# Seven token tiles instead of eight in the first phase of an attention and two-layer kernel, with fewer buffers

## The chip, the cores and the metric

The kernel runs on one core of one Trainium2 chip. The metric is the device time of one execution in microseconds (us), the median of three runs; a profiled execution of its own gives the trace.

## What is computed

The reference in short (float32 in and out; D = 64, 8 heads, 4 batches of 768 positions, so 3072 tokens of 512 values):

```python
for c in range(S // 32):                       # chunks of 32 positions
    k_full = concat(mem_k, k[32c - 16 : 32c + 40])   # 8 memory tokens, 16 left, 8 right
    v_full = concat(mem_v, v[32c - 16 : 32c + 40])
    a = softmax(q_c @ k_full.T / sqrt(64))
    out[32c : 32c + 32] = a @ v_full
x = out as (3072, 512)
h = x @ w_in                                   # 512 -> 2048
g = max(h, 0) + log1p(exp(-abs(h)))            # softplus
x1 = g @ w_out                                 # 2048 -> 512
y = ((x1 @ w_a) * (x1 @ w_b)) @ w_out2         # 512 -> 1536 -> 512
```

## The kernel before, in words

Every matrix product of the two layers is made of three: each operand is split into a high half (rounded to the type that TensorE takes at its full rate) and the low half that is left, and high*high, high*low and low*high are added up.

**Phase 1** makes x1 in token tiles of 384 (`TT`), eight of them. A tile has 16 steps f, one for each 128 columns of w_in. `emit_h` (L563) makes h of the step in 12 matmuls of 384 columns into one of two PSUM banks `ph`. `emit_soft` makes softplus of it: Abs, Exp and Ln on ACT (L570 to L572) in a tile `e`, the sum with max(h, 0) on DVE (L574) into `g`, a ring of two; then `split` writes the high half gh on ACT (L551) and the low half gl on POOL (L554; in the first and the last tile on DVE), each in a ring of three. Two steps later (`LAG`) `emit_x1` (L587) multiplies gh and gl with w_out in 12 matmuls, which add into four accumulator banks `px`. So PE's order is h(f), x1(f-2), h(f+1), x1(f-1), and the last two steps of a tile are multiplied when the next tile's h(0) and h(1) have been made. After the last x1 of a tile the four accumulators are copied to SBUF (L595, tiles `xo`, of which two come from the ring `g`) and stored (L596); the next tile's first product into a bank has to wait for that bank's copy.

**Attention** is done in units of 128 tokens that are woven into phase 1. A unit's steps are: turn (transposes of k and q on DVE, L411 to L414, with copies on ACT), scores (32 small matmuls, L430), soft (eight DVE instructions L379 with eight exps on ACT, L383), norm (DVE L387, L388, then POOL L390), flip and flip2 (five DVE transposes each, L448), values (32 small matmuls, L477) and place (its halves to the x tile, ACT L484 and DVE L485). Each step is put at a slot, a half of a step f, so that a tile has 32: `PLACED` gives the slots at which the three units of a tile have their values, and the other steps are counted from there. The loads of k and q (`HALVES`) are counted from the turns.

**Order.** PE, DVE and SP run in the order in which the program is written out (`order`, `att_at`). ACT and POOL run in the written order in the first and the last tile, and in between in an order that a scheduler chooses. In phase 1 weights of phase 2 are prepared too (`Early`, `Conversion`): `PRE` says how many of such jobs a tile takes.

**Phase 2** works on three pairs of 512 tokens twice, 12 steps each, with seven products of sums (L772, six matmuls of 512 columns each), whose results DVE combines in temporaries q, r and d21 (L824 to L864) in `pair_step`, and the second product as jobs (L795). The first products of phase 2 stand between the last two x1 of phase 1: pX, pY, x1(14), pW, x1(15), pV. pV goes into the bank of the first accumulator. The sums of tokens that the products read (`operand`, `split_hi`, `split_lo`, L652, L656) are in tiles that take over memory of phase 1.

## Time and profile before

| | |
|---|---|
| median of 3 runs | 1172.94 us (1171.99 to 1175.8) |
| the profiled execution's own time | 1173.41 us |
| its span | 1171.6 us |
| PE busy | 1161.1 us, 99% of the span, 7462 instructions |
| DVE busy | 724.2 us, 62% |
| ACT busy | 530.7 us, 45% |
| POOL busy | 263.6 us, 23% |
| chain that ended last | PE 94%, DMA 2%, DVE 1% |

The page gives the busy time of each engine, and the chain of waits says which engine each moment of the span waited for. A matmul is shown with the time until its result is in PSUM, which is longer than the time until the next one may start: the distance of matmuls that follow each other is read from a run of them in the chain. Between two tiles or at the start of a stage the timeline says which instruction ended what wait.

### The profile page before, as it was taken

What the parts mean: (1) busy time and instruction counts of PE and PEld (TensorE: products, weight loads), DVE (VectorE), ACT (ScalarE), POOL (GpSimd) and SP (SyncE); (2) the same over time, 40 slices, a digit from 0 to 9 for tenths busy, and PEclk for the clock granted to TensorE, in tenths of its full rate; (3) what the DMA queues carried; (4) which work ended last, traced back from release to release, by engine and by line L of the source; (5) the groups of instructions that cost most, each with busy time, mean ns of one, the idle gap of its engine ahead of it and who ended that gap; (6) DMA issues with size and microseconds to landing.
All of it is one profiled execution on the core that took longest, in us unless ns stands there. A gap on an engine that the chain in (4) does not pass through costs nothing.

```text
span 1171.6 us, 20283 instructions
## 1 busy us (share of the span) xinstructions
PE 1161.1 (99%) x7462; PEld 1049.1 (90%) x7462; DVE 724.2 (62%) x1603; ACT 530.7 (45%) x1293; POOL 263.6 (23%) x239
## 2 busy tenths in 40 slices
PE   9899999999999999999999999999999999999998
PEld 7799999999999999999999888888888888888887
DVE  6888655565555655455377567867456657455555
ACT  6899666656666566666565332222211113111110
POOL 2000223233232222322324665710002001000000
PEclk9999999999999999999999999999999999999999
DMA  9955353533534335332474758464854443864301
GB/s 228 301 189 103 90 135 76 132 80 98 132 79 125 81 104 136 75 101 68 140 261 161 274 216 287 171 224 150 339 203 144 152 145 106 305 226 153 135 1 72
DMA packets 193714, 181.47 MB, mean 155 GB/s; under 512 B 123168, under 2 KB 151760, under 8 KB 193616
## 3 DMA queue, kind: packets, MB, share of 16 engines
q1 hardware_dynamic: 193232, 180.13, 49.4%
q8 instruction: 59, 0.97, 0.3%
q14 instruction: 39, 0.32, 0.1%
q0 software_dynamic: 384, 0.05, 0.0%
...
## 4 chain that ended last, share of the span: by engine, by line
PE 94%; DMA 2%; DVE 1%; SPq 1%; ACT 0%; issue 0%; POOL 0%; DVEq 0%; POOLq 0%
PE px L587 22%; PE ph L563 22%; PE py L795 17%; PE pX L772 8%; PE pV L772 8%; PE pW L772 8%; PE pY L772 4%; PE pxa L477 2%; PE sc L430 1%; DMA raw<-in_moe_w_in_dram 1%; DMA vv<-in_v_dram 1%; DMA kp<-in_k_dram 1%; SPq L330 1%; DVE af L448 0%; PE pa L466 0%
## 5 line engine op out<-in xcount | busy, mean ns | idle before, releaser
L563 PE MATMUL ph<-x,w 128*128 128x384 f32 x1536 | 289.4, 336 | 0.1
L587 PE MATMUL px<-gh,w 128*128 128x384 f32 x1024 | 281.5, 335 | 1.4 <-DVE qn L295 1.4
L563 PEld LDWEIGHTS ph<-x,w 128*128 128x128 f32 x1536 | 267.2, 188 | 2.1 <-ACT x L369 0.2
L795 PE MATMUL py<-w2o,c 128*128 128x512 f32 (+1 forms) x870 | 218.0, 388 | 0.0
L795 PEld LDWEIGHTS py<-w2o,c 128*128 128x128 f32 x870 | 162.7, 188 | 33.5
L587 PEld LDWEIGHTS px<-gh,w 128*128 128x128 f32 x1024 | 186.7, 188 | 2.8 <-DVE qn L295 1.8
L574 DVE SCALAR_TENSOR_TENSOR g<-ph,e 128x384 f32<-128x384 f32 x128 | 71.0, 555 | 189.0 <-ACT e L572 184.9
L587 PE MATMUL px<-gl,w 128*128 128x384 f32 x512 | 171.1, 334 | 0.0
L854 ACT CAST c<-r 128x512 fp32r<-128x512 f32 x36 | 22.4, 622 | 308.2 <-DVE r L852 287.2
L554 POOL TENSOR_TENSOR gl<-g,gh 128x384 fp32r<-128x384 f32 x96 | 97.3, 1014 | 222.8 <-ACT gh L551 206.7
L551 ACT CAST gh<-g 128x384 fp32r<-128x384 f32 x128 | 65.6, 513 | 88.4 <-DVE g L574 87.2
L804 DVE TENSOR_TENSOR y<-py,y 128x512 f32<-128x512 f32 (+1 forms) x121 | 82.9, 685 | 36.2 <-PE py L795 36.0
L570 ACT ACTIVATE e<-ph 128x384 f32<-128x384 f32 x128 | 62.3, 486 | 88.4 <-PE ph L563 75.7
L587 PEld LDWEIGHTS px<-gl,w 128*128 128x128 f32 x512 | 96.1, 188 | 0.1
L448 DVE STREAM_TRANSPOSE af<-sm 32x256 f32<-32x256 f32 x180 | 78.2, 434 | 3.6 <-POOL sm L390 1.1
L572 ACT ACTIVATE e<-e 128x384 f32<-128x384 f32 x128 | 67.3, 526 | 3.9
L571 ACT ACTIVATE e<-e 128x384 f32<-128x384 f32 x128 | 67.3, 526 | 3.6
L851 DVE TENSOR_TENSOR d<-pW,q 128x512 f32<-128x512 f32 x36 | 24.9, 691 | 69.1 <-PE pW L772 69.1
L383 ACT ACTIVATE sm<-sm,st 128x96 f32<-128x96 f32 x168 | 60.5, 363 | 5.8 <-DVE st L379 5.8
L772 PE MATMUL pX<-x,u 128*128 128x512 f32 x216 | 54.8, 389 | 0.0
L772 PE MATMUL pW<-xs,u 128*128 128x512 f32 x216 | 54.8, 389 | 0.0
L772 PE MATMUL pY<-xs,u 128*128 128x512 f32 x216 | 54.8, 389 | 0.0
...
## 6 DMA issues: line engine op xcount, KB each, us to landing
...
```

Of the source, the lines that this page charges most:

```text
L448: nc.vector.transpose(out=af[32 * kb:32 * kb + 32, x], in_=self.sm[32 * x:32 * x + 32, :, 32 * kb:32 * kb + 32])
L551: anchor[0] = nc.scalar.copy(hi, val)
L554: engine.tensor_tensor(lo, val, hi.bitcast(F32), ALU.subtract)
L563: nc.tensor.matmul(ph, lhsT=w[:, a, kt * P:(kt + 1) * P], rhs=x[:, c, kt, :], start=n == 0, stop=n == 3 * KT - 1)
L570: nc.scalar.activation(e, ph, AF.Abs)
L571: nc.scalar.activation(e, e, AF.Exp, scale=-1.0)
L572: nc.scalar.activation(e, e, AF.Ln, bias=1.0)
L574: nc.vector.scalar_tensor_tensor(g, ph, 0.0, e, ALU.max, ALU.add)
L587: nc.tensor.matmul(acc[t][i][:, :TT], lhsT=a, rhs=c, start=f == 0 and m == 0, stop=f == NF1 - 1 and m == 2)
L772: nc.tensor.matmul(bank[:, :T2], lhsT=u[:, j, a, kt * P:kt * P + P], rhs=x[kt][:, c], start=first_ and m == 0, stop=m == 3 * KH - 1, skip_ ...
L795: nc.tensor.matmul(b, lhsT=c[:, x, r], rhs=w[:, y, cols], start=n == 0, stop=n == 3 * GROUP - 1)
L804: tt(y, b, y, ALU.add)
```

## The change

The last 1536 tokens of phase 1 are cut into three tiles of 512 instead of four of 384, so that there are seven tiles. The units get a list of 18 slots with even distances, 9 in the narrow tiles and 8 in the wide ones, and where the distance is under 9 the flips come one slot earlier. Softplus is finished in place in `e`, a ring of two, and `g` is gone; gh and gl are rings of two, and both halves of a step are now made behind x1(f-2), the last reader of the buffers that they take. Of the accumulators' copies two go to the ring `e` and two to a tag that the early jobs use. In phase 2 the sums s1 and 12 share one tile and 22 and s4 another, and the temporaries r and d21 are two halves of a tile `rd` that takes over the memory of the ring gl. `order` splits the sums at other places. The diff, cut to its core:

```diff
 T2 = 512
+WIDTHS = (384, 384, 384, 384, 512, 512, 512)
 
 LAG = 2
-PLACED = (11, 21, 30)
+PLACED = (43, 52, 61, 70, 79, 88, 97, 106, 116, 126, 134, 142, 150, 158, 166, 174, 182, 190)
 TURNED, SCORED = 32, 34
 TURN, SOFT, NORM, FLIP, FLIP2 = -2, 1, 3, 5, 6
-HALVES = ((0, 8, 0.6), (8, 13, 0.9))
+HALVES = ((0, 8, 0.6), (8, 13, 0.8))
 SETS = 1
...
 
-PRE, PRE_BY = 5, 4.2
+PRE, PRE_BY = (0, 5, 5, 6, 7, 7, 0), 4.2
 PRE_STEPS = (0, 3.4, 4.1, 4.3)
...
 
-    masks = [ap.tile([P, KB], F32, name=f"mask{i}") for i in range(4)]
+    masks = [ap.tile([P, KB], F32, name=f"mask{i}") for i in range(3)]
+    masks.append(wp.tile([P, KB], F32, tag="w", name="mask3"))
     ident = wp.tile([P, P], F32, tag="w", name="ident")
...
         if t not in xt:
-            xt[t] = mp.tile([P, 2, KT, TT], F32R, tag="x", name=f"x{t}")
+            xt[t] = mp.tile([P, 2, KT, T2], F32R, tag="x", name=f"x{t}")[:, :, :, :WIDTHS[t]]
         return xt[t]
...
             mask = masks[0 if self.n == 0 else 2 if self.n == NU - 1 else 1]
-            sm = a2.tile([P, H, KB], F32, tag="sm", name=f"sm{u}", bufs=1)
-            st = a2.tile([P, 4, H], F32, tag="st", name=f"st{u}")
+            sm = a2.tile([P, H, KB], F32, tag="kt", name=f"sm{u}", bufs=1)
+            st = a2.tile([P, 4, H], F32, tag="st", name=f"st{u}", bufs=1)
             softmax(self.sc, mask, sm, st)
...
     later = units[UPT:]
-    placed = {u: 2 * NF1 * (u // UPT - 1) + PLACED[u % UPT] for u in range(2 * UPT, len(units))}
+    placed = dict(zip(range(2 * UPT, len(units)), PLACED))
     scored = {u: placed[u - 1] if u > 2 * UPT else SCORED for u in placed}
...
         whens[i] = [(turned[u], "turn"), (at - 0.005, "scores"), (at + SOFT, "soft"), (at + NORM, "norm"),
-                    (max(at + FLIP, to - 7), "flip"), (max(at + FLIP2, to - 5), "flip2"), (to - 0.03, "values"), (to - 0.02, "place")]
+                    (at + FLIP - (to - at < 9), "flip"), (at + FLIP2 - (to - at < 9), "flip2"), (to - 0.03, "values"), (to - 0.02, "place")]
         unit.own_bank = u + 1 < len(units)
...
         if tag not in rings:
-            rings[tag] = mp.tile([P, n, TT], dtype, tag=tag, name=tag, bufs=1)
+            rings[tag] = mp.tile([P, n, T2], dtype, tag=tag, name=tag, bufs=1)
             n_turn[tag] = 0
         n_turn[tag] += 1
         return rings[tag][:, n_turn[tag] % n]
 
-    def split(val, name, engine=nc.gpsimd, between=None):
-        hi, lo = turn_of("gh", 3, F32R), turn_of("gl", 3, F32R)
-        anchor[0] = nc.scalar.copy(hi, val)
-        if between:
-            between()
-        engine.tensor_tensor(lo, val, hi.bitcast(F32), ALU.subtract)
-        return hi, lo
-
     def emit_h(t, f):
         x, w = xt[t], w1[f]
-        ph = ps.tile([P, 512], F32, tag="h", name=f"ph{t}_{f}")[:, :TT]
+        ph = ps.tile([P, 512], F32, tag="h", name=f"ph{t}_{f}")[:, :WIDTHS[t]]
         n = 0
...
     def emit_soft(t, f, ph, engine=nc.gpsimd, one=None, two=None):
-        e = mp.tile([P, TT], F32, tag="e", name=f"e{t}_{f}")
+        c = slice(0, WIDTHS[t])
+        e = turn_of("e", 2, F32)[:, c]
+        hi, lo = turn_of("gh", 2, F32R)[:, c], turn_of("gl", 2, F32R)[:, c]
         nc.scalar.activation(e, ph, AF.Abs)
         nc.scalar.activation(e, e, AF.Exp, scale=-1.0)
         nc.scalar.activation(e, e, AF.Ln, bias=1.0)
-        g = turn_of("g", 2, F32)
-        nc.vector.scalar_tensor_tensor(g, ph, 0.0, e, ALU.max, ALU.add)
+        nc.vector.scalar_tensor_tensor(e, ph, 0.0, e, ALU.max, ALU.add)
         if one:
             one()
-        gt[t, f] = split(g, f"g{t}_{f}", engine, two)
+        gt[t, f] = hi, lo
+
+        def parts():
+            anchor[0] = nc.scalar.copy(hi, e)
+            if two:
+                two()
+            engine.tensor_tensor(lo, e, hi.bitcast(F32), ALU.subtract)
+
+        return parts
 
...
             for m, (a, c) in enumerate(((wh, gh), (wh, gl), (wl, gh))):
-                nc.tensor.matmul(acc[t][i][:, :TT], lhsT=a, rhs=c, start=f == 0 and m == 0,
+                nc.tensor.matmul(acc[t][i][:, :WIDTHS[t]], lhsT=a, rhs=c, start=f == 0 and m == 0,
                                  stop=f == NF1 - 1 and m == 2)
+
+    def emit_x1_out(t, f):
         if f == NF1 - 1:
             for i in range(KT):
+                n = WIDTHS[t]
                 if t == NTILE - 1:
-                    o = wp.tile([P, TT], F32, tag="w", name=f"xo{t}_{i}")
+                    o = wp.tile([P, n], F32, tag="w", name=f"xo{t}_{i}")
+                elif i > 1:
+                    o = mp.tile([P, n], F32, tag="tmp", name=f"xo{t}_{i}", bufs=2)
                 else:
-                    o = turn_of("g", 2, F32) if i > 1 else mp.tile([P, TT], F32, tag="e", name=f"xo{t}_{i}")
-                nc.vector.tensor_copy(o, acc[t][i][:, :TT])
-                nc.sync.dma_start(x1d[:, i, TT * t:TT * t + TT], o)
+                    o = turn_of("e", 2, F32)[:, :n]
+                nc.vector.tensor_copy(o, acc[t][i][:, :n])
+                nc.sync.dma_start(x1d[:, i, C0[t]:C0[t + 1]], o)
             del acc[t]
...
         if n in ("11", "s2", "s3"):
-            return [home(f"x{n}", late["x"], [P, KH, 2, T2], f"x{n}")]
-        if n == "s1":
-            return [home("xs1a", late["x"], [P, 1, 2, T2], "xs1"), home("xa", mp, [P, 3, 2, T2], "x")[:, 0:1]]
-        if n == "12":
-            return [home("xa", mp, [P, 3, 2, T2], "x")[:, 1:3]]
-        if n == "22":
-            return [home("xb", mp, [P, 3, 2, T2], "x")[:, 0:2]]
-        return [parts[p, "xb"][:, 2:3], home("xs4b", mp, [P, 1, 2, T2], "gh")]
-
-    def pieces_of(p, n):
-        k = 0
-        for x in sums[p, n]:
-            yield x, raws[n][:, k:k + x.shape[1]]
-            k += x.shape[1]
-
-    def split_hi(p, n, copy):
-        sums[p, n] = operand(p, n)
-        for x, raw in pieces_of(p, n):
-            copy(x[:, :, 0], raw)
-
-    def split_lo(p, n, engine):
-        for x, raw in pieces_of(p, n):
-            engine.tensor_tensor(x[:, :, 1], raw, x[:, :, 0].bitcast(F32), ALU.subtract)
+            return home(f"x{n}", late["x"], [P, KH, 2, T2], f"x{n}")
+        x = home("xa" if n in ("s1", "12") else "xb", mp, [P, 4, 2, T2], "x")
+        return x[:, 0:2] if n in ("s1", "22") else x[:, 2:4]
+
+    PIECES = {n: 1 for n in PRODUCTS}
+
+    def split_hi(p, n, copy, which=(0, 1)):
+        for i in which:
+            if i < PIECES[n]:
+                x = operand(p, n, i)
+                sums.setdefault((p, n), []).append(x)
+                k = x.shape[1]
+                copy(x[:, :, 0], raws[n][:, i * k:i * k + k])
+
+    def split_lo(p, n, engine, which=(0, 1)):
+        for i in which:
+            if i < PIECES[n]:
+                x = sums[p, n][i]
+                k = x.shape[1]
+                engine.tensor_tensor(x[:, :, 1], raws[n][:, i * k:i * k + k], x[:, :, 0].bitcast(F32), ALU.subtract)
 
...
     def temp(tag, name):
-        return mp.tile([P, T2], F32, tag=tag, name=name, bufs=2 if tag == "e" else 1)
+        if tag == "e":
+            return turn_of("e", 2, F32)
+        if "t2" not in late:
+            late["t2"] = mp.tile([P, 2, T2], F32, tag="gl", name="rd", bufs=1)
+        return late["t2"][:, 0 if tag == "g" else 1]
 
...
         pre = [Early(*divmod(n, 3)) for n in range(3 * NF2)]
-        n_pre = PRE * (NTILE - 2)
-        for n, e in enumerate(pre[:n_pre]):
-            t, i = divmod(n, PRE)
+        n_pre = sum(PRE)
+        for n, (t, i) in enumerate((t, i) for t in range(NTILE) for i in range(PRE[t])):
+            e = pre[n]
             for d, step in zip(PRE_STEPS, (e.fetch, e.top, e.value, e.store)):
-                plan.append((2 * NF1 * (t + 1) + PRE_BY * i + d, 100 + n, step))
+                plan.append((2 * NF1 * t + PRE_BY * i + d, 100 + n, step))
         plan.sort(key=lambda p: p[:2])
```

Three places in the order of the instructions, from the built programs (the numbers behind names are those of buffers).

DVE where tile 2 begins, in the kernel before (ph2_1 is h of tile 2, step 1; px1_0 to px1_3 are the accumulators of tile 1; sm9 is the weights of attention unit 9):

```order
L574 SCALAR_TENSOR_TENSOR g_660<-ph2_1_2660,e2_1_2673 128x384
L595 COPY xo1_0_2694<-px1_0_1861 128x384
L595 COPY xo1_1_2697<-px1_1_1862 128x384
L595 COPY g_660<-px1_2_1863 128x384
L595 COPY g_660<-px1_3_1864 128x384
L574 SCALAR_TENSOR_TENSOR g_660<-ph2_2_2704,e2_2_2717 128x384
L448 STREAM_TRANSPOSE af_83<-sm9_2601 32x256 x5
```

The same place in the changed kernel:

```order
L571 SCALAR_TENSOR_TENSOR e_656<-ph2_1_2629,e_656 128x384
L451 STREAM_TRANSPOSE af_83<-sm9_2557 32x256 x5
L605 COPY e_656<-px1_0_1840 128x384
L605 COPY e_656<-px1_1_1841 128x384
L605 COPY xo1_2_2669<-px1_2_1842 128x384
L605 COPY xo1_3_2672<-px1_3_1843 128x384
L451 STREAM_TRANSPOSE af_83<-sm9_2557 32x256 x5
L571 SCALAR_TENSOR_TENSOR e_656<-ph2_2_2680,e_656 128x384
L414 STREAM_TRANSPOSE kt10_2698<-kn_78 128x8x64
```

The first five transposes of a flip stand ahead of the four copies of the accumulators now, and the next unit's turn (kt10) follows behind g(2,2). Tiles 4 and 5 begin in the same way, with five transposes ahead of the copies; at tile 3 the eight softmax pieces of unit 13 stand there.

ACT around the start of tile 2, in the kernel before:

```order
L551 CAST gh_666<-g_660 128x384
L383 ACTIVATE sm9_2601,st9_2602<-sm9_2601,st9_2602 128x96 x8
L570 ACTIVATE e2_0_2632<-ph2_0_2619 128x384
L571 ACTIVATE e2_0_2632<-e2_0_2632 128x384
L572 ACTIVATE e2_0_2632<-e2_0_2632 128x384
L551 CAST gh_666<-g_660 128x384
L570 ACTIVATE e2_1_2673<-ph2_1_2660 128x384
L571 ACTIVATE e2_1_2673<-e2_1_2673 128x384
```

And in the changed kernel:

```order
L577 CAST gh_657<-e_656 128x384
L386 ACTIVATE sm9_2557,st9_2558<-sm9_2557,st9_2558 128x96 x8
L568 ACTIVATE e_656<-ph2_0_2593 128x384
L569 ACTIVATE e_656<-e_656 128x384
L570 ACTIVATE e_656<-e_656 128x384
L568 ACTIVATE e_656<-ph2_1_2629 128x384
L577 CAST gh_657<-e_656 128x384
L569 ACTIVATE e_656<-e_656 128x384
```

The cast of gh(2,0) stood ahead of the next step's Abs and stands behind it now.

DVE at the start of phase 2, in the kernel before, with the engines whose semaphores are waited for:

```order
L554 TENSOR_TENSOR gl_667<-g_660,gh_666 128x384 [waits PE_49,Activation_49]
L824 TENSOR_TENSOR q0_0_7499<-pY0_0_7505,q0_0_7499 128x512 [waits PE_49,Activation_49]
L656 TENSOR_TENSOR xb_0_7503<-x22_0_7066,xb_0_7503 128x2x512 [waits Activation_49]
L835 TENSOR_TENSOR r0_0_7538<-pW0_0_7531,q0_0_7499 128x512 [waits DVE_49,PE_49]
L595 COPY xo7_0_7558<-px7_0_6947 128x384 [waits PE_49]
```

And in the changed kernel:

```order
L580 TENSOR_TENSOR gl_658<-e_656,gh_657 128x512 [waits Activation_49]
L835 TENSOR_TENSOR e_656<-pY0_0_6862,e_656 128x512 [waits PE_49,Activation_49]
L663 TENSOR_TENSOR xb_0_6860<-x22_0_6437,xb_0_6860 128x2x512 [waits Activation_49]
L846 TENSOR_TENSOR rd_6895<-pW0_0_6888,e_656 128x512 [waits DVE_49,PE_49]
L605 COPY xo6_0_6913<-px6_0_6314 128x512
```

The wait for PE that the last gl had is gone from it, since gl stands behind the cast now. r is written to rd, whose memory is that of gl, so that its wait for PE is one for the last product that reads gl; the copy of the first accumulator stands behind it as before.

## Rows read from the trace of the kernel before

**Rows 1.** Windows: us, busy (x) of PE, PEld, DVE, ACT, POOL, clock, DMA share, GB/s.

```profile
422.00:495.00 73.00, 73.00 (x578) 71.69 (x577) 41.28 (x127) 45.91 (x127) 20.50 (x19) 1.00 0.42 103
640.00:1171.00 531.00, 528.17 (x2336) 437.53 (x2335) 326.19 (x462) 112.03 (x196) 104.94 (x78) 1.00 0.52 185
```

**Rows 2.** Chain of waits, phase 1: start us, us, what.

```profile
292.42 1.08 PE pxa L477 x32
293.50 0.82 PE sc L430 x32
294.32 2.31 PE ph L563 x12
296.63 2.08 PE px L587 x12
```

**Rows 3.** Chain of waits, phase 2: one product.

```profile
1140.90 1.36 PE pV L772 x6
```

**Rows 4.** Timeline, tile 3 to tile 4: start us, us, engine, instruction [idle before, releaser].

```profile
345.30 1.47 POOL L390 TENSOR_TENSOR sm<-sm,st 128x768 f32<-128x768 f32 x1 [4.75 <-DVE st L388]
...
346.50 0.33 PE L587 MATMUL px<-gh,w 128*128 128x384 f32 x1
...
348.40 0.56 DVE L574 SCALAR_TENSOR_TENSOR g<-ph,e 128x384 f32<-128x384 f32 x1 [3.25 <-ACT e L572]
...
348.88 1.01 DVE L595 COPY xo<-px 128x384 f32<-128x384 f32 x2
...
349.00 0.51 ACT L551 CAST gh<-g 128x384 fp32r<-128x384 f32 x1 [0.69 <-DVE g L574]
...
349.59 1.01 POOL L554 TENSOR_TENSOR gl<-g,gh 128x384 fp32r<-128x384 f32 x1 [1.84 <-ACT gh L551]
...
350.66 0.33 PE L587 MATMUL px<-gh,w 128*128 128x384 f32 x1
...
351.45 0.49 ACT L570 ACTIVATE e<-ph 128x384 f32<-128x384 f32 x1 [1.94 <-DMA x_scratch<-xo]
```

**Rows 5.** Timeline, DVE, five pieces of a flip in tile 4.

```profile
353.56 2.22 DVE L448 STREAM_TRANSPOSE af<-sm 32x256 f32<-32x256 f32 x5
```

**Rows 6.** Timeline, a unit's turn: first and last DVE instruction.

```profile
313.69 0.70 DVE L411 STREAM_TRANSPOSE kt<-kn 128x512 f32<-128x512 f32 x1
...
314.64 0.67 DVE L414 STREAM_TRANSPOSE qt<-qn 128x512 f32<-128x512 f32 x1
```

**Rows 7.** Timeline, one unit's softmax: first and last DVE piece, last exp on ACT.

```profile
56.13 0.25 DVE L379 CUSTOM_DVE_ANT_0 sm<-sc,mask 128x96 f32<-128x96 f32 x1
...
57.37 0.25 DVE L379 CUSTOM_DVE_ANT_0 sm<-sc,mask 128x96 f32<-128x96 f32 x1
...
58.95 0.36 ACT L383 ACTIVATE sm<-sm,st 128x96 f32<-128x96 f32 x1
...
59.43 0.17 DVE L387 TENSOR_SCALAR st<-st 128x8 f32<-128x8 f32 x1 [0.67 <-ACT sm L383]
```

**Rows 8.** The page's part 5: 384 against 512 columns, DVE and ACT.

```profile
L574 DVE SCALAR_TENSOR_TENSOR g<-ph,e 128x384 f32<-128x384 f32 x128 | 71.0, 555 | 189.0 <-ACT e L572 184.9
...
L854 ACT CAST c<-r 128x512 fp32r<-128x512 f32 x36 | 22.4, 622 | 308.2 <-DVE r L852 287.2
...
L551 ACT CAST gh<-g 128x384 fp32r<-128x384 f32 x128 | 65.6, 513 | 88.4 <-DVE g L574 87.2
...
L851 DVE TENSOR_TENSOR d<-pW,q 128x512 f32<-128x512 f32 x36 | 24.9, 691 | 69.1 <-PE pW L772 69.1
```

**Rows 9.** Timeline, start of phase 2: DVE's last copies and PE's first product.

```profile
631.54 0.69 DVE L835 TENSOR_TENSOR r<-pW,q 128x512 f32<-128x512 f32 x1 [1.60 <-PE pW L772]
...
632.15 2.03 DVE L595 COPY xo<-px 128x384 f32<-128x384 f32 x4
...
633.08 0.33 PE L587 MATMUL px<-gl,w 128*128 128x384 f32 x1
...
633.42 0.86 PE L772 MATMUL pV<-xs1a,u 128*128 128x512 f32 x3
```

More of the change, by code (lines that the diff above doesn't have):

```diff
@@ L66, in attn_moe_moe2 @@
     UPT = TT // QU
+    C0 = [sum(WIDTHS[:t]) for t in range(len(WIDTHS) + 1)]
     BPT = TT // QB
     KS = KB // 32
-    NTILE = NT // TT
+    NTILE = len(WIDTHS)
     NPAIR = NT // (2 * T2)
@@ L480, in place @@
         def place(self):
-            t, c0 = divmod(self.u * QU, TT)
+            t = sum(self.u * QU >= c for c in C0[1:])
+            c0 = self.u * QU - C0[t]
             x = x_tile(t)
@@ L526, in attn_moe_moe2 @@
             plan.append((dict((step, at) for at, step in whens[i])["values"] + 0.015, i, later[i + SETS].load_v))
-    for t in range(2, NTILE):
+    for t in range(2, NT // TT):
         for lo, hi, by in HALVES if t > 2 else ((0, NP + 1, 0.25),):
@@ L624, in add_pair, with operand @@
             engine.tensor_tensor(r["s4"], r["12"], r["s2"], ALU.subtract)
-    def operand(p, n):
+    def operand(p, n, i):
         def home(key, pool, shape, tag):
@@ L978, in order @@
                     convert()
-                    emit_soft(t, f, ph, nc.vector, convert)
-                    convert()
+                    parts_ = emit_soft(t, f, ph, nc.vector, convert, convert)
                 elif t < NTILE - 1:
-                    emit_soft(t, f, ph)
+                    parts_ = emit_soft(t, f, ph)
                 else:
-                    emit_soft(t, f, ph, nc.vector, partial(slot, 2 * f), partial(slot, 2 * f + 1))
+                    parts_ = emit_soft(t, f, ph, nc.vector, partial(slot, 2 * f), partial(slot, 2 * f + 1))
                 att_at(2 * (NF1 * t + f))
-                if len(pend) >= LAG:
-                    emit_x1(*pend.pop(0))
+                done = pend.pop(0) if len(pend) >= LAG else None
+                if done:
+                    emit_x1(*done)
+                parts_()
+                if done:
+                    emit_x1_out(*done)
                 pend.append((t, f))
@@ L990, in between_0 @@
         def between_0():
-            emit_x1(*pend.pop(0))
+            emit_x1(*pend[0])
+            emit_x1_out(*pend.pop(0))
         for k in sorted(plan2):
             slot(k)
+        V, G = nc.vector, nc.gpsimd
+        HIGHS = (("11",),), (("s2",),), (("s3",),), (), (("s1",),), (("12",),), (("22",),)
+        LOWS = (), (("11", V),), (("s2", G),), (("s3", V),), (), (("s1", V),), (("12", G),)
+        HIGHS_0 = ("s4",), (), (), (), (), (), ()
+        LOWS_0 = (("22", V),), (("s4", V),), (), (), (), (), ()
         for p in range(NPAIR):
@@ L1027, in at @@
                         if f == NF2 - 1:
-                            split_hi(p + 1, PRODUCTS[k], nc.scalar.copy)
-                            if k > 0:
-                                split_lo(p + 1, PRODUCTS[k - 1], nc.gpsimd if k in (2, 4) else nc.vector)
-                    if f == 0 and k == 0 and p > 0:
-                        split_lo(p, PRODUCTS[6], nc.vector)
-                    if p == f == 0 and k in (0, 2):
-                        split_hi(0, PRODUCTS[5 + k // 2], nc.scalar.copy)
-                    if p == f == 0 and k in (1, 3):
-                        split_lo(0, PRODUCTS[5 + k // 2], nc.vector)
+                            for n, *which in HIGHS[k]:
+                                split_hi(p + 1, n, nc.scalar.copy, which or (0, 1))
+                            for n, engine in LOWS[k]:
+                                split_lo(p + 1, n, engine)
+                    if f == 0 and p > 0:
+                        for n in HIGHS_0[k]:
+                            split_hi(p, n, nc.scalar.copy)
+                        for n, engine in LOWS_0[k]:
+                            split_lo(p, n, engine)
+                    if p == f == 0:
+                        if k == 0:
+                            split_hi(0, "22", nc.scalar.copy)
+                        if k == 1:
+                            split_lo(0, "22", nc.vector)
+                        if k == 2:
+                            split_hi(0, "s4", nc.scalar.copy)
+                        if k == 3:
+                            split_lo(0, "s4", nc.vector)
                 pair_step(p, f, at, (between_0, between_0) if (p, f) == (0, 0) else ())
```

## The prediction

> **What bounds the kernel now.** I read the windows first, one of a tile in the middle of phase 1 and one of most of phase 2. In the first PE is busy for 73.00 of 73.00 us, in the second for 528.17 of 531.00 [rows 1]. DVE, ACT and POOL are busy for 41, 46 and 21 us of the tile. So PE is the bound without a gap, at a granted clock of 1.00. A change gains only by taking time out of PE's own row of matmuls, and loses what it puts between them as a wait. That is why the chain is read next, for the price of a matmul, and then the timeline at the places where the order of the other engines changes.
>
> **The price of a matmul.** In the chain twelve matmuls of 384 columns take 2.08 us, 173.3 ns each [rows 2]; six of 512 columns in phase 2 take 1.36 us, 226.7 ns each [rows 3]. At the upper of the clock's two levels, 2.4 GHz, 384 columns are 160.0 ns and 512 are 213.3, so both rows leave 13.3 ns over, whatever the width.
>
> **What the change takes away.** h and x1 are 12 + 12 matmuls a step and 16 steps a tile. Four tiles of 384 are 4 x 16 x 24 = 1536 matmuls, or 266.2 us by 173.3 ns; three tiles of 512 are 1152, or 261.1 us by 226.7. **PE's own work falls by 5.1 us** (384 x 13.3 ns). All of it lies on the path. Units, early jobs (30 as before) and phase 2 keep their work on PE.
>
> **What a tile's first product waits for.** This is where the order was changed most. Before, at the start of tile 4, h(4,1) ends at 346.50, where x1(3,15) begins; DVE's g follows at 348.40 and the first two copies of the accumulators at 348.88, 1.01 us together; the next tile's first product starts at 350.66 [rows 4]. So the first copy lands at 348.88 + 0.51 = 349.39. With the 0.04 to 0.08 us that rows 4 show between one engine's end and the next one's start (the cast after g, POOL after the cast), taken as 0.07, it could have let the product start at 349.46, which is 1.2 us early. PE hides the copy. In the changed order other work stands between g(t,1) and that copy:
> - Tile 2: five transposes of a flip, 2.22 us [rows 5], minus 1.2: a stall of 1.0. Two more things come to it there. On ACT the cast of gh(2,0) has gone behind Abs of step 1, which can put the cast's 0.51 us, or nothing, into the way of g(2,1): I take 0.4. And the store of the first copy now empties a half of the ring e, into which Abs(2,2) writes: before, ACT waited until 351.45 for such a store, 2.1 us after the copy [rows 4]. Counted from the end of h(2,1), the copy ends at 2.9 + 2.2 + 0.4 = 5.5, Abs starts at 7.6, g(2,2) is done 2.5 us later (346.50 to 348.96 in rows 4), and the turn of unit 10 stands behind it on DVE with 1.62 us (313.69 to 315.31) [rows 6], so it ends near 11.7. PE wants that unit's scores after x1(1,15), h(2,2), x1(2,0), h(2,3) and the values before them, 4 x 2.08 + 1.08 [rows 2] and the 1.4 us already waited, at 10.8. Flips overlap with the waiting, so this is 0.9 at most and nothing at least; I take 0.5. **Together 1.9.**
> - Tile 3: the eight DVE pieces of a unit's softmax, 56.13 to 57.55, 1.42 us [rows 7], minus 1.2: **0.2**.
> - Tile 4: five transposes again, but h(4,1) is 512 wide. Casts of 512 columns against 384 take 622 against 513 ns on ACT, and DVE's additions 691 against 555 [rows 8], so three activations and g are 3 x 0.11 + 0.14 = 0.47 later. The copy (still of 384) lands at 2.89 + 0.07 + 0.47 + 2.22 = 5.65 after h(4,1); PE comes to it after x1(3,15), 2.08, and a wide h(4,2), 12 x 0.227 = 2.72, at 4.80. **0.85.**
> - Tile 5: the copy is wide too (+0.14, 5.79), and so is x1(4,15): 5.44. **0.35.**
> - Tiles 1 and 6: no step of a unit stands there. In the last tile DVE makes gl itself behind the cast, which comes after x1(5,15): 2.72 + 0.62 + 0.69 + 0.64 + 3 x 0.07 = 4.88, before 5.44. Nothing.
>
> **The start of phase 2.** Before, r was written at 631.54, while x1 still ran, and the four copies from 632.15 on, 0.51 us each; pV followed x1 at 633.42 without a gap [rows 9]. In the change r takes the memory of gl and has to wait for the last product that reads it, which is the last but one of x1(15) (its counterpart starts at 633.08, and ends with the block). Then r and the first copy run behind each other in front of pV: 0.07, then 0.61 from r to the copy, then 0.51 + 0.13 for a wide copy, then 0.07, less 0.06 as gl's last product is two places before the end: **1.33**. That is the surest of the stalls, as PE has nothing else in its order there.
>
> **What costs nothing.** The cast of gh(f) now waits for x1(f-2). In a step with a unit, counted from the end of h(f): values and scores take 1.90 us of PE [rows 2]; softmax runs from the scores' end + 0.2 for 3.18 us on DVE and ACT (56.13 to 59.31 in rows 7), to 5.3; then the cast, beside about 0.6 for two small DVE instructions (59.43 the first) and POOL's norm of 1.47 [rows 4], to 7.4; then gl, 1.01, **8.4**. x1(f) starts after x1(f-2), h(f+1), x1(f-1), h(f+2), the unit, and the 0.23 by which the first matmuls after it are longer (2.31 against 2.08 in rows 2): 4 x 2.08 + 2.13 = **10.4**. 2.0 us hide it; if they were gone, each us would cost six times over in the narrow tiles (the units whose softmax falls there ahead of the cast). In wide tiles both sides grow, to 9.9 against 13.0. The fetches of k and q stand behind the turns as before, with some three slots, over 6 us, left; phase 2's sums change homes and split places by steps of one product and keep their number. SP issues 28 stores of x1 for 32. The first tile's reordering leaves PE's order alone.
>
> **The sum.** Stalls 1.9 + 0.2 + 0.85 + 0.35 + 1.33 = 4.6; gain 5.1; net -0.5, on the profiled execution's 1173.4 (span 1171.6 and 1.8 around it), which lies 0.5 over the median of 1172.9. I predict **1172.5**: the change gives back at six places what it takes out of PE's row. With tile 2's two estimates at nothing and each of the five stalls 0.2 less it is 1170.5; with 0.51 and 0.9 there and each stall 0.3 more, 1174.5.
>
> **Rivals.**
> - *Slower: the rings of two.* One mechanism: a cast or gl that comes late starves x1(f). Place: the narrow tiles with a unit's exps ahead of the cast, six of them. It decides when over 2.0 us more get ahead of gl(f): the early jobs' work on ACT (a cast like L854's 0.62), the next step's three activations (1.9, 346.50 to 348.40 in rows 4) and the turn's copies could, if the scheduler's order and the real times differ. With 2.7 more, 0.7 x 6 = 4.2 on top: 1176.7. For it speaks that ACT, 63% busy in a tile [rows 1], bunches its work there; against it, that one late step is caught up by the next. Chance 0.13.
> - *No gain per matmul.* If what a matmul costs over its columns grew with them in phase 1, 512 columns would take 4/3 of 173.3 = 231.1 ns, nothing would be saved, and the stalls would stand alone: 1172.9 + 4.6 = 1177.5. Rows 3 speak against it, with another product's 226.7. Chance 0.05. The Trainium skill (TensorE: Matmul & The Clock Gate, "Wait — 56ns, not 53.3ns?") states a fixed cost of about 2.5 ns a matmul when warm; by that, 384 fewer would save 1.0 us and the sum would be 1176.6. The trace has 13.3 at both widths and disagrees with it.
> - *Faster: the copies aren't late.* If the flips are done before g(t,1) lets them wait, since DVE is 57% busy [rows 1], only the start of phase 2 stays: 1172.9 - 5.1 + 1.3 = 1169.1. Against it: the order puts the flips behind g and not ahead of it. Chance 0.10.
>
> **How the numbers follow.** The forecast has 0.72, and its own range, 1170.5 to 1174.5, lies within 0.3% (3.5 us, about what a measurement of this kernel can tell from no change). Slower is 0.13 + 0.05 = 0.18, faster 0.10. The range reaches down to the faster rival and up over the first slower one, 1169.0 to 1177.0; what is left out is the second one and the tails.
>
> **What would show it.** In the changed trace, twelve wide matmuls of phase 1 in 2.72 us; PE's wait before the first product of tiles 2, 3, 4 and 5, released by DVE's copy, of 1.0 to 1.5, 0.2, 0.85 and 0.35 us; one wait before the scores of unit 10; one before pV of 1.3, released by the copy; none elsewhere. The forecast is wrong if x1 waits for gh or gl within tiles (the first rival), if wide matmuls take over 2.75 a dozen (the second), or if the copies let PE go on (the third).

## The result and the profile after

The changed kernel takes **1184.73 us** (median of 6 runs, 1182.76 to 1186.66) against 1172.59 for the kernel before; the ratio is **1.0099, interval 1.0082 to 1.0115**. It is 12 us slower, and outside the range that was given. The profiled execution has a span of 1183.9 us against 1171.6, 12.3 more.

First the page's part 1 of the changed kernel, then one piece of its chain of waits, in a tile of 512:

```profile
PE 1161.6 (98%) x7078; PEld 1002.3 (85%) x7078; DVE 731.3 (62%) x1578; ACT 517.4 (44%) x1224; POOL 256.7 (22%) x221
```

```profile
397.41 2.72 PE ph L559 x12
```

Twelve wide matmuls take 2.72 us, 226.7 ns each, as [rows 3] said: the gain is there, 384 matmuls fewer and 5.1 us. PE's busy time has not fallen all the same (1161.6 us against 1161.1); the end of this section says why. And the gain is eaten by waits of PE, which a view by what was waited for lists (us in total, times, longest):

```profile
PE sc L433 <- DVE qt L417: 4.7, 6, 2.1
...
PE pxa L480 <- DVE e L571: 2.5, 5, 1.0
PE px L592 <- DVE qn L298: 2.2, 2, 1.3
...
PE pxa L480 <- DVE af L451: 1.1, 1, 1.1
PE sc L433 <- ACT kt L419: 0.7, 1, 0.7
```

The same view of the kernel before has these two of them:

```profile
PE px L587 <- DVE qn L295: 1.4, 1, 1.4
...
PE sc L430 <- DVE qt L414: 1.0, 1, 1.0
```

**The waits that were forecast** stand where they should, in the timeline of PE (the bracket is the wait): the first products of tiles 2, 3, 4 and 5, the scores of unit 10, and pV.

```profile
209.31 0.41 PE L592 MATMUL px<-gh,w 128*128 128x384 f32 x1 [1.26 <-DVE e L605]
...
215.09 0.89 PE L433 MATMUL sc<-kt,qt 64*64 64x96 f32 x32 [0.30 <-DVE qt L417]
...
292.73 0.41 PE L592 MATMUL px<-gh,w 128*128 128x384 f32 x1 [0.16 <-DVE e L605]
...
370.53 0.47 PE L592 MATMUL px<-gh,w 128*128 128x512 f32 x1 [0.82 <-DVE e L605]
...
466.68 0.47 PE L592 MATMUL px<-gh,w 128*128 128x512 f32 x1 [0.31 <-DVE e L605]
...
645.81 1.65 PE L779 MATMUL pV<-xa,u 128*128 128x512 f32 x6 [1.16 <-DVE xo L605]
```

Together 4.0 us, where 4.6 were forecast. **What was not forecast** lies at the attention units of the narrow tiles. Slot 52, ACT, DVE and PE:

```profile
159.89 0.67 ACT L688 ACTIVATE raw_a<-raw_a 128x512 f32<-128x512 f32 x1
...
161.57 0.56 DVE L571 SCALAR_TENSOR_TENSOR e<-ph,e 128x384 f32<-128x384 f32 x1 [2.70 <-ACT e L570]
162.04 2.22 DVE L451 STREAM_TRANSPOSE af<-sm 32x256 f32<-32x256 f32 x5
164.29 0.43 DVE L692 TENSOR_SCALAR val_a<-raw_a 128x512 uint32<-128x512 uint32 x1
164.75 0.69 DVE L693 SCALAR_TENSOR_TENSOR val_a<-raw_a,val_a 128x512 uint32<-128x512 uint32 x1
165.48 2.23 DVE L451 STREAM_TRANSPOSE af<-sm 32x256 f32<-32x256 f32 x5
167.74 0.56 DVE L571 SCALAR_TENSOR_TENSOR e<-ph,e 128x384 f32<-128x384 f32 x1
...
168.35 1.15 PE L480 MATMUL pxa<-af,vn 96*64 96x64 f32 x32 [1.02 <-DVE e L571]
169.98 1.09 PE L433 MATMUL sc<-kt,qt 64*64 64x96 f32 x32 [0.48 <-DVE qt L417]
```

DVE does g, half a flip, the value of an early job (1.1 us), the other half, the next g and, from 168.22 on, the turn, without a pause. The values are written to a bank of the ring that h uses; the g at 167.74 is the last reader of that bank. So PE waits 1.02 us for g, and then 0.48 for the turn behind it. The kernel before has the same row on DVE, with the early job's value in it, and no wait:

```profile
162.01 0.67 ACT L681 ACTIVATE raw_a<-raw_a 128x512 f32<-128x512 f32 x1
...
163.72 0.43 DVE L685 TENSOR_SCALAR val_a<-raw_a 128x512 uint32<-128x512 uint32 x1
...
167.24 0.56 DVE L574 SCALAR_TENSOR_TENSOR g<-ph,e 128x384 f32<-128x384 f32 x1
...
169.31 1.15 PE L477 MATMUL pxa<-af,vn 96*64 96x64 f32 x32
```

There the unit stands at slot 53, and PE comes to its values 2 us later. The second difference is on ACT: the early job's own step (raw_a, 0.67 us) stands ahead of the Exp and Ln of the row's first g now, where it stood behind them, and that g starts 2.56 us after its h instead of 2.02. Slot 88 has the same row on DVE, and waits of 0.54 and 0.67 us.

At slots 106 and 116 (0.8 and 0.7 us) ACT is what comes late. It waits for the load of an early job there (the bracket), with a step of softplus behind it; at slot 116 DVE has a value in the row too.

```profile
303.48 0.67 ACT L688 ACTIVATE raw_o<-raw_o 128x512 f32<-128x512 f32 x1 [1.59 <-DMA raw_o<-in_moe_w_out_dram]
...
322.76 0.67 ACT L688 ACTIVATE raw_b<-raw_b 128x512 f32<-128x512 f32 x1 [3.06 <-DMA raw_b<-in_moe_w_b_dram]
```

The four slots make 4.2 us. Slot 79 has such a load in its most costly form. SP, ACT and PE:

```profile
227.69 0.39 SPq L681 DMA_DIRECT2D raw_b<-in_moe_w_b_dram  x1
...
231.52 0.67 ACT L688 ACTIVATE raw_b<-raw_b 128x512 f32<-128x512 f32 x1 [4.12 <-DMA raw_b<-in_moe_w_b_dram]
...
232.08 0.48 ACT L568 ACTIVATE e<-ph 128x384 f32<-128x384 f32 x1
...
236.58 0.69 PE L480 MATMUL pxa<-af,vn 96*64 96x64 f32 x16 [1.05 <-DVE af L451]
239.40 1.56 PE L433 MATMUL sc<-kt,qt 64*64 64x96 f32 x32 [2.13 <-DVE qt L417]
240.88 4.21 PE L559 MATMUL ph<-x,w 128*128 128x384 f32 x12
```

On SP an early job's load of raw_b now stands behind loads of k and q that begin at 217.17; before, it was issued at 217.68, ahead of those from 218.71 on. ACT has that job's step in its order ahead of the next Abs and waits 4.12 us for the load; softplus, flips, turn, values and scores are late behind it, 3.2 us on PE.

Between 140 and 348 us ACT waits for such loads six times, 0.8 to 4.1 us; in the kernel before the view shows no such wait.

And the last row shows a cost that no list of waits has: twelve h matmuls take 4.21 us, where this view has 2.24 for the twelve at 160.93. After the pauses at slots 52 and 79 the granted clock is at 1.2 GHz, the lower of its two levels, for a while (0.50 from 240 to 244 us). Two windows hold these stretches (length, busy time of PE, PEld, DVE, ACT, POOL, then the clock):

```profile
166.00:176.00 10.00, 8.50 (x93) 7.85 (x92) 5.39 (x12) 3.75 (x9) 1.60 (x2) 0.83 0.52 119
...
230.00:247.00 17.00, 13.82 (x116) 13.10 (x115) 6.71 (x14) 7.59 (x16) 1.99 (x2) 0.80 0.57 136
```

10 x 0.17 + 17 x 0.20 = 5.1 us of matmul time; this is why PE's busy time did not fall. **The sum**: 4.0 forecast + 4.2 at four units + 3.2 for raw_b + 5.1 for the clock + 1.2 in the first tile (two waits for qn of 2.2 instead of one of 1.4, and one of 0.45 at 96 us) - 0.2 at slot 43 = 17.5, less 5.1 gained: 12.4, against 12.3 of the spans. That it fits so closely is in part luck. PE's first steps came 1.0 us earlier in this execution (a product ptq at 45.28 against 46.27), which the sum leaves out, so about as much in small pieces is missing from it as well.

### The profile page after: what moved, and what is told of

Its sections match the earlier page's. It is cut to its first block, busy times and chain, and to the rows that moved or that the text cites. A ratio compares the mean times of both kernels' runs of the same rounds, so it can differ in the third digit from the quotient of the medians.

```text
span 1183.9 us, 19390 instructions
## 1 busy us (share of the span) xinstructions
PE 1161.6 (98%) x7078; PEld 1002.3 (85%) x7078; DVE 731.3 (62%) x1578; ACT 517.4 (44%) x1224; POOL 256.7 (22%) x221
## 4 chain that ended last, share of the span: by engine, by line
PE 84%; DVE 5%; DMA 4%; ACT 3%; SPq 2%; issue 1%; POOL 0%; DVEq 0%; ACTq 0%; POOLq 0%
PE px L592 18%; PE ph L559 17%; PE py L806 17%; PE pV L779 8%; PE pX L779 8%; PE pW L779 8%; PE pY L779 4%; DVE af L451 2%; PE sc L433 1%; PE pxa L480 1%; DMA raw_b<-in_moe_w_b_dram 1%; DMA kp<-in_k_dram 1%; SPq L333 1%; DMA raw<-in_moe_w_in_dram 1%; ACT e L569 1%
## 5 line engine op out<-in xcount | busy, mean ns | idle before, releaser
L559 PE MATMUL ph<-x,w 128*128 128x384 f32 (+1 forms) x1344 | 285.3, 361 | 0.1
L592 PE MATMUL px<-gh,w 128*128 128x384 f32 (+1 forms) x896 | 270.5, 363 | 4.8 <-DVE e L605 2.6
L571 DVE SCALAR_TENSOR_TENSOR e<-ph,e 128x384 f32<-128x384 f32 (+1 forms) x112 | 68.7, 613 | 199.7 <-ACT e L570 199.2
L592 PE MATMUL px<-gl,w 128*128 128x384 f32 (+1 forms) x448 | 161.3, 360 | 0.0
L580 POOL TENSOR_TENSOR gl<-e,gh 128x384 fp32r<-128x384 f32 (+1 forms) x80 | 91.2, 1140 | 257.1 <-ACT gh L577 252.5
L568 ACT ACTIVATE e<-ph 128x384 f32<-128x384 f32 (+1 forms) x112 | 59.6, 532 | 106.1 <-PE ph L559 89.3
L577 ACT CAST gh<-e 128x384 fp32r<-128x384 f32 (+1 forms) x112 | 62.4, 558 | 68.7 <-DVE e L571 48.1
L569 ACT ACTIVATE e<-e 128x384 f32<-128x384 f32 (+1 forms) x112 | 63.9, 570 | 3.2
L570 ACT ACTIVATE e<-e 128x384 f32<-128x384 f32 (+1 forms) x112 | 63.9, 571 | 3.1
L779 PE MATMUL pV<-xa,u 128*128 128x512 f32 x216 | 55.0, 390 | 1.2 <-DVE xo L605 1.2
L779 PE MATMUL pX<-xa,u 128*128 128x512 f32 x216 | 54.9, 390 | 0.0
```

Source lines behind the costliest of these rows:

```text
L559: nc.tensor.matmul(ph, lhsT=w[:, a, kt * P:(kt + 1) * P], rhs=x[:, c, kt, :], start=n == 0, stop=n == 3 * KT - 1)
L569: nc.scalar.activation(e, e, AF.Exp, scale=-1.0)
L570: nc.scalar.activation(e, e, AF.Ln, bias=1.0)
L571: nc.vector.scalar_tensor_tensor(e, ph, 0.0, e, ALU.max, ALU.add)
L577: anchor[0] = nc.scalar.copy(hi, e)
L580: engine.tensor_tensor(lo, e, hi.bitcast(F32), ALU.subtract)
```

## The experiments

Times are medians; the ratio is to the kernel before, measured beside it.

**Which part costs?** e1 has the change's buffers with the widths, slots and jobs of before, e9 only the change's slots.

```diff
 e1: -WIDTHS = (384, 384, 384, 384, 512, 512, 512)
     +WIDTHS = (384,) * 8        # and PLACED, PRE, HALVES, flips of before
 e9 (in the kernel before):
     +placed.update(zip(range(6, 16), (43, 52, 61, 70, 79, 88, 97, 106, 116, 126)))
```

> The change's buffers and orders (softplus in place, rings of two, sums' homes, r in gl's memory) with the widths, units and early jobs of the kernel before (eight tiles of 384). Theory 1, order on the queues (units 9 slots apart bring flips, an early job's value and the next turn together on DVE, and k/q loads ahead of an early job's raw_b on SP): no wait of PE within tiles beyond those of before, only the one before pV, so 1172.6 + 1.2, i.e. 1173.5 to 1175. Theory 2, the rings of two starve x1 or hold softplus: several waits of PE in each tile of 384 also here, 1178 or more, and a fallen clock somewhere.

> The kernel before (eight tiles of 384, rings of three, early jobs as they were) with nothing but the change's ten slots of the narrow stretch, 43 to 126, for the units 6 to 15; the others stay. Theory 1, the units 9 slots apart are what DVE can't keep up with: waits before values and scores at slots 52, 79, 88, 106 and 116 as in the changed kernel, 4 to 8 us and perhaps a stretch at half clock: 1177 to 1181. Theory 2, the rings of two and softplus in place cause them: no such waits, within 1 us of before.

e1: 1179.15, ratio 1.0050 (1.0032 to 1.0068). One wait of 0.2 us at a unit beyond those of before, which speaks against starved rings, but the time is 6.3 us longer and not 1.2. In its profile, 5.7 longer: 1.1 before pV; 0.7 and 0.45 in the first tile; 0.3 at the start of each of the tiles 2 to 6, 1.5 together; 0.7 more until 47 us, where PE waits 1.2 for kn, a wait that the change and e2 with the same start have with 0 and 0.8; the rest are pieces of 0.1 to 0.3. The 0.3 is this (POOL, DVE, PE at 352 us):

```profile
352.40 1.02 POOL L580 TENSOR_TENSOR gl<-e,gh 128x384 fp32r<-128x384 f32 x1 [1.74 <-ACT gh L577]
...
353.45 0.56 DVE L605 COPY e<-px 128x384 f32<-128x384 f32 x1 [1.33 <-POOL gl L580]
...
353.71 0.80 PE L592 MATMUL px<-gh,w 128*128 128x384 f32 x2
```

The second accumulator's copy has its new home in the ring e and waits for gl of step 1, that half's last reader; PE waits for the copy (two products take 0.80 instead of 0.51). ACT waits for early jobs' loads here too, up to 3.1 us, but with the units' slots of before no unit's product pays for it.

e9: 1177.74, ratio 1.0037 (1.0020 to 1.0055). The slots alone bring the waits into a kernel with rings of three:

```profile
166.73 1.15 PE L477 MATMUL pxa<-af,vn 96*64 96x64 f32 x32 [0.56 <-DVE g L575]
168.35 0.89 PE L430 MATMUL sc<-kt,qt 64*64 64x96 f32 x32 [0.48 <-DVE qt L414]
...
206.14 0.41 PE L588 MATMUL px<-gh,w 128*128 128x384 f32 x1 [1.28 <-DVE xo L596]
...
253.47 1.15 PE L477 MATMUL pxa<-af,vn 96*64 96x64 f32 x32 [0.56 <-DVE g L575]
...
255.29 0.89 PE L430 MATMUL sc<-kt,qt 64*64 64x96 f32 x32 [0.67 <-DVE qt L414]
```

The time is as expected, the places are so in part. The units' list makes the waits at slot 52 (1.0 of the 1.5 us; raw_a stands behind the g on ACT here, as before), all of those at slot 88 and the copies' wait at tile 2. Slots 79, 106 and 116, clear or nearly clear here, need the rest of the change as well.

**The single causes.** e2 puts the copies ahead of what stood before them, e3 moves loads of k and q, e4 the early jobs of the narrow tiles (their loads move with their values), e5 gives r a tile of its own.

```diff
 e2: -att_at(2 * (NF1 * t + f))     # for t > 1, f == 1: called behind emit_x1_out
 e3: +at += 3.6 * (t == 4 and lo == 0)
 e4: +VALUE_AT = (36.1, 41.3, 46.2, 51.2, 55.4, 60.3, 64.5, 69.2, ... 105.2)
 e5: +late["r"] = late["x"].tile([P, T2], F32, tag="r", name="r", bufs=1)
```

> The change, with the accumulators' copies ahead of the flip or softmax pieces that stood before them at tiles 2 to 5. Theory 1: the four waits of x1 for the copies (1.26, 0.16, 0.82, 0.31 in the changed profile) go, nothing else changes much: 1184.7 - 2.5 = 1182.2. If those waits only hide a later one (flips late, then values or scores late), under 1 us is won.

1188.7, ratio 1.0129 (1.0114 to 1.0145): a miss, 4 us worse than the change. The waits for copies at tile 2 fall from 1.3 to 0.3, and those for values grow there, since flips and turn now come later:

```profile
209.65 0.44 PE L592 MATMUL px<-gh,w 128*128 128x384 f32 x1 [0.28 <-DVE e L605]
...
215.56 1.15 PE L480 MATMUL pxa<-af,vn 96*64 96x64 f32 x32 [1.98 <-DVE e L571]
```

The same happens at tiles 3, 4 and 5. DVE has too much to do in that stretch; its order only decides who waits.

> The change, with the first k and q loads for the units 12 and 13 put 3.6 slots later, so that SP issues raw_b ahead of them. Theory 1: raw_b lands before ACT wants it, the waits of 1.05 and 2.13 us before values and scores at slot 79 go and with them the 6.8 us at half clock that follow (3.4 us lost): 1184.7 - 6.6 = 1178. Theory 2 (rings): those waits are softplus coming late by itself, and stay: 1184 to 1185.

1181.56, ratio 1.0064 (1.0040 to 1.0087). At slot 79 values start without a wait and scores with 0.17 instead of 2.13 us: the load of raw_b was the cause. Only about 3 of the 6.6 us show in the median, as the clock falls behind slot 88 instead (0.89 from 250 to 266 us in the profile); the four executions run from 1177.5 us at a mean granted clock of 1.000 to 1182.8 at 0.997.

> The change, with the values of the early jobs in the narrow tiles moved out of the stretches between a unit's flips and the next turn. Theory 1: the waits at slots 52, 88 and 116 (1.50, 1.21, 0.67 us) fall to under 0.3 each, and the 3.4 us at half clock after slot 52 (1.7 us lost) go: 1184.7 - 4.5 = 1180; raw_b's wait at slot 79 stays or moves. Theory 2: the waits stay, 1184 to 1185.

1177.51, ratio 1.0040 (1.0025 to 1.0054): 7 us of the 12, more than expected, but not from where it was expected. Slot 52 still waits 0.90 and 0.48 us, slot 88 still 1.0. The waits at slots 106 and 116 are gone, and that at slot 79 falls from 3.2 to 0.6, as the jobs' loads have moved too. The largest part is the clock, which stays at 1.00 throughout, though those 1.4 us at slot 52 and one wait of 1.8 at tile 2 are left. At slot 52 the value has only moved ahead of the first g, and there it takes 3.1 us instead of 1.1:

```profile
158.78 1.67 DVE L693 TENSOR_SCALAR val_o<-raw_o 128x512 uint32<-128x512 uint32 x1 [0.23 <-issue]
160.48 1.39 DVE L694 SCALAR_TENSOR_TENSOR val_o<-raw_o,val_o 128x512 uint32<-128x512 uint32 x1
```

POOL works on the unit's norm and on gl at that time (158.69 to 161.31).

> The change, with r of phase 2 in a tile of its own instead of in gl's memory. The prediction's step: PE's one wait before pV, 1.16 us after the change, goes and nothing takes its place: about 1.2 us less than the change, 1183.5. Rival: pV waits for the copy of the accumulator anyway, since the copies are wide now, and 0.6 us or more of the wait stay.

One execution: 1185.24, span 1183.4. Those of the change lie between 1182.76 and 1186.66, so the time can't show 1 us, but the trace can: pV follows x1 without a wait.

```profile
645.47 1.52 PE L779 MATMUL pV<-xa,u 128*128 128x512 f32 x6
```

**Early jobs or even slots?** e6 to e8, e10 and e11 changed slots, flips and jobs together, and none came to the time hoped for.

```diff
 e6:  +PLACED = (43, 53, 62, 71, 80, 89, 98, 107, 117, 126, 134, ...)   # with e4's values and e5
 e7:  e6 with e3's loads
 e8:  -(to - at < 9)    +(to - at < 10)     # both flips; with e4's values and e5
 e10: +PLACED = (..., 126, 135, 143, 151, 158, 167, 175, 183, 190), values between flips at odd slots
 e11: e10 with e3's loads
```

> The change with three edits: early values apart as in e4, r apart as in e5, and the narrow tiles' units at 43, 53, 62, 71, 80, 89, 98, 107, 117, 126, so that fewer of them stand at even slots and no flip or softmax stands ahead of the copies at tiles 2 and 3. Theory 1 (DVE's order decides): e4's 1177.5 less 1.2 for pV, less 1.9 for the copies' wait at tile 2, less about 2 for the waits at slots 52 and 88: 1172 to 1173, no half clock. Theory 2 (rings of two): waits for gl or gh within tiles appear in the same sum, over 1175.

> As e6, and the first k and q loads of units 12 and 13 3.6 slots later as in e3. Theory 1: SP's raw_b no longer stands behind the loads; where e6 still waits at its slot 80 (its kt or qt late), up to 1 us less than e6; no difference if the early jobs' new places have taken that wait away already.

> The change with its own slots, early values apart as in e4, r apart as in e5, and the flips of units 9 slots apart one slot earlier (4 and 5 behind the scores, as the wide tiles have them). Theory 1: at the even slots values and scores no longer wait (1.4 + 1.1 us in e4), tile 2's copies wait for flip2 rather than flip: 1173 to 1175. Rival: the flips come before POOL's norm is done, DVE waits for it with g behind, and x1 waits for gh: no better than e4.

> The change with r apart, units at 43, 53, 62, 71, 80, 89, 98, 107, 117, 126, 135, 143, 151, 158, 167, 175, 183, 190 (no flip or softmax ahead of the copies at the tiles 2 to 5) and each early value put where DVE waits anyway, 1.5 slots behind a unit's scores, or between the flips of units whose values stand at an odd slot. Theory 1: at most 0.5 us of waits at any unit, none for the copies, none before pV: 5.1 gained less 1.2 in the first tile and 1 to 2 elsewhere: 1170 to 1171.5. Theory 2: waits of 1 us at even slots stay: 1174 or more.

> As e10, and the first k and q loads of units 12 and 13 3.6 slots later. Theory 1: where e10 still waits for a raw part or a turn around slot 80, up to 2 us less than e10; otherwise the same within 0.5.

e6: 1178.75 (1.0036 to 1.0068), with a wait of 1.0 for g and 0.48 for the turn at each even slot, 62, 80 and 98, where a value stood ahead of norm, and two waits of h itself for a g, 0.8 and 1.6. e7, 1180.54 (1.0040 to 1.0081), was expected at or below it; it has the same waits at slot 80, so the loads had no part in those. e8: 1185.5 (1.0076 to 1.0124): both flips stand ahead of the copies at tile 2, PE waits 4.2 us there. e10: 1181.82 (1.0044 to 1.0095): values between flips cost 1.1 at the scores of odd slots too, and the two units that stand 7 slots apart in the wide tiles cost 4.5; e11: 1184.61 (1.0056 to 1.0111), the same waits and more time at the lower clock. The next two tell it apart: jobs taken out of the narrow tiles, with the change's own slots (e12) or e6's (e13).

```diff
 e12: -PRE, PRE_BY = (0, 5, 5, 6, 7, 7, 0), 4.2
      +PRE, PRE_BY = (0, 3, 4, 3, 10, 10, 0), 3.08        # with e5's r
      +PRE_STEPS = (0, 2.5, 3.1, 3.25)
      +VALUE_AT = (35.5, 44.5, 53.5, 62.5, 71.5, 80.5, 89.5, 98.5, 107.5, 117.5)   # 1.5 behind the scores
 e13: e12 with e6's slots, the values moved along;  e14: e13 with wide slots 135, 143, ... 191
```

> The change with its own slots, r apart, and ten early jobs instead of sixteen in the narrow tiles, each value 1.5 slots behind a unit's scores (the wide tiles take twenty instead of fourteen). Theory 1a, the early values are what DVE lacks time for: at the slots 52, 70, 79, 88, 106 and 116 at most 0.3 us of wait remains each, only the four waits for the copies stay (2.5 us): 1173 to 1174. Theory 1b, the even slots alone are too tight with the rings of two: 0.5 + 0.48 us stay at each even slot, four to five of them, 1176 to 1178.

> As e12 with the narrow units at 43, 53, 62, 71, 80, 89, 98, 107, 117, 126, the wide ones as the change has them. Theory 1a: the copies wait at tiles 4 and 5 only (1.1 us): 1170 to 1172. Theory 1b: waits at the even slots 62, 80 and 98, 1 us each: 1173 to 1175.

> As e13 with the wide units at 135, 143, ... 191, so that their flips stand behind the copies. Gains the 1.1 us of the copies' waits and loses about 0.6 where x is placed right ahead of the first h of tile 5 and 1.4 at tile 6: within 1 us of e13. It tells whether waits for copies come back elsewhere in wide tiles, as e2's did.

e12: 1177.39, ratio 1.0040 (1.0025 to 1.0054), and the question is settled by its trace. Slot 52, which waited 1.5 us:

```profile
166.82 1.15 PE L481 MATMUL pxa<-af,vn 96*64 96x64 f32 x32
167.91 0.89 PE L434 MATMUL sc<-kt,qt 64*64 64x96 f32 x32
```

No unit of the list waits any more in the narrow tiles but unit 10 with 0.3, with the same even slots and rings of two. So the wait takes both, an even slot and an early job in the row: before had the job without the slot, e12 has the slot without the job. A job costs 1.1 us of DVE between a unit's softmax and the next turn, and 0.67 of ACT. e12 takes both away and doesn't tell them apart; e9, with the value in the row and ACT's step behind the g, waits 0.56 for g where the change waits 1.02. The time is higher than expected, as with twenty jobs the units of the wide tiles wait some 4 us, in rows like this:

```profile
389.76 0.89 PE L434 MATMUL sc<-kt,qt 64*64 64x96 f32 x32 [0.67 <-DVE qt L418]
```

e13: 1176.76, ratio 1.0028 (1.0015 to 1.0040): the copies' waits at tiles 2 and 3 are gone too, the wide tiles wait as in e12. e14 (1178.51, 1.0029 to 1.0070) gained nothing: the wait at tile 4 goes, the units of the wide tiles wait longer, like e2's.

**Is the width's gain to be had?** e15 places thirty values by hand, 1.5 slots behind a unit's scores or just behind its turn, sixteen of them in the wide tiles; e16 moves the flips ahead of the wide tiles' copies behind them; e17 has eleven in the narrow tiles, seventeen in the wide ones and eight instead of six in the last.

```diff
 e17: +PRE, PRE_BY = (0, 5, 5, 5, 7, 6, 0), 4.2        # with e6's slots and e5
      +VALUE_AT = (35.5, 41.3, 44.5, 54.5, 63.5, 72.5, 81.5, 90.5, 99.5, 108.5, 118.5,
      +            127.5, 132.3, 135.5, 140.3, 143.5, 148.3, ... 183.5, 187.3, 190.5)
      +plan2.setdefault(2 + 3 * n + d, []).append(step)    # last tile
```

> As e13 (r apart, narrow units at 43, 53, 62, 71, 80, 89, 98, 107, 117, 126), with all thirty early values put by hand, 1.5 slots behind a unit's scores or just behind its turn: fourteen in the narrow tiles, sixteen in the wide. Theory 1a: the narrow tiles stay without waits as in e13, and the wide ones lose the waits that e13's ten jobs a tile brought (some 6 us); left are the copies at tiles 4 and 5 (1.1 us), 1.9 in the first two tiles and 0.6 at slot 71: 1176.8 - 5.5 = 1171, 2.5 under before. Theory 1b: waits at units come back in one of the two, 1174 or more.

> As e15, with the flips of the two units that stand ahead of the copies at tiles 4 and 5 one slot later, behind the copies. Gains 1.1 us if nothing takes the place of these waits, 1170; as e2's copies did, the later flips may make the next scores wait 0.4 us or more, then no difference.

> As e15 without the four early values behind turns at the slots 51, 69 and 87 and in the wide tiles' last unit as they were: eleven jobs in the narrow tiles, seventeen in the wide ones, and eight instead of six in the last tile. Theory 1a (each further early value within a unit's steps in a narrow tile costs 0.5 to 1.5 us of PE's waits): the waits of e15 at slots 58 to 62, 71, 79 and 89 (some 4 us) go: 1173.2 - 4 = 1169.5, 3 under before. If the last tile can't take two more jobs, waits appear there or before pX to pV, and less is won.

e15: 1173.24, ratio 1.0009 (0.9999 to 1.0019), level with before; the three values just behind turns that e17 leaves out cost 2.9 us of waits, three of them x1's for POOL's gl, 0.4 each. e16: 1181.07 (1.0058 to 1.0089), 2.1 and 2.2 us at two units for the 1.1 at the copies, and the clock falls behind the second (0.83 from 464 to 474 us). **e17: 1170.12, ratio 0.9968 (0.9956 to 0.9980), 3.9 us faster than the kernel before** and faster than all others. Part 1 of its page, and of its list of waits those behind the start:

```profile
PE 1155.6 (99%) x7078; PEld 997.1 (85%) x7078; DVE 736.4 (63%) x1578; ACT 518.5 (44%) x1224; POOL 256.0 (22%) x221
```

```profile
PE px L594 <- DVE qn L300: 1.5, 2, 1.3
...
PE px L594 <- DVE e L607: 1.1, 2, 0.8
PE sc L435 <- DVE qt L419: 0.6, 1, 0.6
PE pxa L482 <- DVE e L573: 0.5, 1, 0.5
...
PE px L594 <- POOL gl L582: 0.2, 1, 0.2
```

PE is busy for 5.5 us less than before; the waits are 3.9 us against before's 2.4, and 1.1 of them are the copies at tiles 4 and 5. e17 differs from the kernel before in more than the width (buffers, units, jobs), so the 3.9 us are those of the whole; the fall in PE's busy time is the one that the width was to bring.

## Why the prediction was wrong

- **What bounds the kernel, the price of a matmul, the gain:** right. 226.7 ns and 5.1 us are in the trace, and e17's busy time shows them. The Trainium skill's fixed cost of 2.5 ns a matmul (TensorE: Matmul & The Clock Gate, "Wait — 56ns, not 53.3ns?") would have given 1.0 us, as an estimate; the trace has 13.3 ns over the columns at 512 in phase 1 too.
- **The copies, unit 10's scores and pV:** right in place and size, 1.26, 0.16, 0.82, 0.31, 0.30 and 1.16 us against 1.0 + 0.4, 0.2, 0.85, 0.35, 0.5 and 1.33. e5 shows that r's home was pV's cause. Not costed: a copy in the ring e that waits for gl, 0.3 us a tile (e1).
- **"What costs nothing" is the step that failed.** It weighed gh and gl against x1(f), found 2.0 us, and this holds: PE nowhere waits for gh or gl in the changed kernel. But it set the units' new slots and the early jobs at nothing without asking the same of the *unit's own* products. The counting is short: at slot 52 h(8) ends about 159.0; PE comes to the values after x1, h, x1 and h, 8.3 us later; ACT's share takes 2.6 (0.5 of it for raw_a), then DVE needs 0.56 + 2.22 + 1.12 + 2.23 + 0.56, together 9.3. That is the 1.0 us of the row. Without the early job it fits, as e12 shows, and a slot later, where the kernel before had the unit, it fits with the job. Slots 52 and 88 cost 2.7 us by this.
- **"The fetches of k and q stand behind the turns as before"** looked at their own due time alone. Behind them on SP stands raw_b, ahead of Abs on ACT (3.2 us; e3). The late loads at slots 106 and 116 (1.4 us) are of the same kind; no run moves them alone.
- **"The first tile's reordering leaves PE's order alone":** true of PE's order, but on DVE gl now stands between copies of qn, and x1 waits for such a copy twice (0.91 and 1.28 us) instead of once (1.45); a g is 0.45 late at 96 us. 1.2 us together. In e10 and e17, with the same first tile, the waits for qn are 1.3 and 1.5, so part of it varies from run to run.
- **The clock** was in no term: 5.1 us on top of two pauses. The range had no room for waits that bring a slower clock after them.
- The first rival named the narrow tiles with exps ahead of the cast, and a loss of 0.7 us at six units, but by another mechanism: gh and gl were never late in the changed kernel. One of its grounds, early jobs' work on ACT, had its part at slots 52, 79, 106 and 116. Where jobs were moved, x1 did wait for gl (e4 0.8 us once, e8 0.6 and 0.8, e15 to e17 0.2 to 0.4 each). The second and the third fell with the trace.

Open is what makes the loads late at slots 106 and 116: e1, without the slots, has such waits of ACT, e9, with the slots alone, hardly any (0.27 us), so the change's other orders bring them and the slots make them costly, but which order does is not shown. Open is also how far the pieces of 0.1 to 0.3 us in e1 come from the buffers.
